# 64 of 512 columns of a copied score bank's exponential as a power of two times a polynomial, on VectorE and GpSimd

## The chip, the core and the metric

The kernel runs on one core of one Trainium2 chip. The metric is device microseconds of one execution: 1353.58 us for the kernel before, the median of three runs (1353.39 to 1354.35). The profile is of a further execution of the same kernel, taken by the hardware profiler; its own time is 1347.44 us, and its span, from the first to the last instruction, is 1345.6 us. Engines are named as in the profile: PE (TensorE matmul), PEld (TensorE weight load), ACT (ScalarE), DVE (VectorE), POOL (GpSimd), SP (SyncE, which here issues most DMAs).

## The reference

The output is a gated mix of a softmax attention and a mixture of experts over the same 2048 tokens of width 448. Only the attention's inner part is touched by the change.

```python
def _A_ref(x, wqkv, wo):                       # B = 1, S = 2048, D = 448, H = 16, Dh = 28
    q, k, v = ...
    scores = jnp.einsum("bhqd,bhkd->bhqk", q, k) * scale      # scale = Dh ** -0.5
    p = _softmax(scores, axis=-1)
    o = jnp.einsum("bhqk,bhkd->bhqd", p, v)
    return ...(o) @ wo

def _B_ref(x, w_gate, w1, w2):                 # 8 experts, the best 2 of each token
    ...

g = _sigmoid((x * gate_w).sum(-1, keepdims=True))
return g * _A_ref(x, A_wqkv, A_wo) + (1 - g) * _B_ref(x, B_w_gate, B_w1, B_w2)
```

## The kernel before

The kernel has four stages one after the other. First the projections, the routing of tokens and a pass of query-key products that finds each query's largest score; then the eight experts (to about 833 us in the profile), beside which that pass of maxima goes on; then attention (to about 1306 us); then the output projection of the 16 blocks of 128 tokens, which is the tail.

**Units and steps.** Attention is cut into 16 units u: four groups g of four heads by four chunks qc of 512 queries. A unit has eight steps p, and a step takes two blocks of 128 keys for the four heads at once. So there are 128 steps m = 8u + p. For each of the two key blocks, `score_passes` (L733) runs three passes of four matmuls, one for each head in rows of its own of the array, into four PSUM banks of 128 keys by 512 queries. The query carries minus its largest score as an extra row, so the scores come out shifted and the exponential needs no further bias. Three of the four banks are one tile (`s0` for the first key block, `s1` for the second), the fourth is a single bank, `z0` or `z1` in turn.

**The exponentials of a step.** In `scores(m)` ACT takes the first block's single bank (L1173, 512 columns) and its triple (L1174, 1536 columns) straight from PSUM. The second block's single bank is copied to SBUF first, by DVE (L1175, tile `X`), which frees the bank early; ACT then takes the second triple (L1176) and last the copy (L1177, 512 columns from `X`). All eight results stand in `P`. ACT does nothing else in this stage.

**The sums.** `values(m)` multiplies the eight parts of `P` by the values (L1188) into a single bank, the one that `z0` of the next step's scores has just left; row 28 of each head's 32 is the sum of the exponentials. DVE adds the bank to `osb` (L1194, and L1192 where p is 0). That same bank is then the second single bank of the scores after.

**The order.** PE, ACT, DVE and POOL follow the order in which the code is written; SP's DMAs stand in its own queue in the order in which they are issued. The loop issues `scores(m + 1)`, then `beside(m)`, then `values(m)`. So on DVE a step is: the copy of step m+1, the operations of `beside(m)`, the sum of step m.

**What `beside` adds.** At p = 2, 4, 5, 6 one DVE operation of `routed` (L1073 twice, L1075, L1077), which combines the experts' rows of one token block; at p = 5 two gathers by POOL for the next unit (L1064). The unit before is finished in between: at p = 0 `collect_sums` writes the four sum rows to DRAM and reads them back as 128x16 (L1110, L1112); at p = 3 `invert_sums` takes the reciprocal on DVE (L1116) and writes it (L1117); at p = 4 `spread_sums` reads it back, spread over 32 rows for each head (L1122); at p = 7 `divide` multiplies `osb` by it (L1127) and sends the rows to `OT` by SP (L1137). These small DMAs are issued by POOL. At p = 0 of the units 5 to 8 DVE also splits a block of `wo` (L1057, L1058), and at p = 0, 1 and 3 of unit 15 a block of `OT` (L1086 and the helper's L180, L181). The keys, values and queries of what comes next are loaded by SP: a unit's queries at p = 7 of two units before (L719, L721), a group's keys at p = 3 and p = 6 of the last unit of the group before (L704, L707), its second half of values at p = 0 of its first unit (L691).

**The tail.** Each of the 16 blocks needs 22 matmuls (L1097), one DVE operation (L1100) and a DMA to the output; ACT and DVE split `OT` four blocks ahead. The last unit's sums are collected, inverted, spread and divided between these blocks, and blocks 12 to 15 need them.

Of the kernel before, what the change touches and what calls it, by code (L numbers as in the profile page):

```python
# [1 line left out]

# [6 lines left out]
F32 = mybir.dt.float32  # L9
F32R = mybir.dt.float32r  # L10
BF = mybir.dt.bfloat16
I32 = mybir.dt.int32
AF = mybir.ActivationFunctionType
ALU = mybir.AluOpType
# [21 lines left out]
S, D, H, DH, E, FF = 2048, 448, 16, 28, 8, 1792  # L36
# [13 lines left out]
SCALE = float(DH) ** -0.5  # L50
# [7 lines left out]
def bc(ap, shape):  # L58
    return ap.to_broadcast(shape)
# [3 lines left out]
def tile_gated_mha_moe(ctx: ExitStack, tc: tile.TileContext, x, xe_, xT, wv, wqk, wo, w1, w2, out):  # L63
    nc = tc.nc
# [10 lines left out]
    sum_d = dram.tile([NG * 4, 4, 512], F32, name="sum_d")  # L75
    inv_d = dram.tile([NG * 4, 4, 512], F32, name="inv_d")
# [200 lines left out]
    with ExitStack() as pa:  # L277
        sb = pa.enter_context(tc.tile_pool(name="pa_sb", bufs=1))
# [116 lines left out]
        for t in range(NT):  # L395
# [11 lines left out]
            if 7 <= t < 15:  # L407
                b, c = divmod(t - 7, 2)
# [3 lines left out]
                                        op=ALU.subtract)  # L412
# [325 lines left out]
    with ExitStack() as pb:  # L738
        sb1 = pb.enter_context(tc.tile_pool(name="pb_sb1", bufs=2, reuse_waits="tile"))
        sb = pb.enter_context(tc.tile_pool(name="pb_sb", bufs=2, reuse_waits="tile"))  # L740
# [159 lines left out]
        for e in range(E):  # L900
# [12 lines left out]
            for hf in range(2):  # L913
# [3 lines left out]
                for f in range(NH):  # L917
                    ft = hf * NH + f
                    p = e * NP + ft // 2
# [69 lines left out]
                for n_k, k in enumerate((4, 0, 1, 2, 3)):  # L989
# [12 lines left out]
                    for f in range(NH if k < 4 else 0):  # L1002
# [10 lines left out]
                        if hf == 1 and e + 1 < E and (f == 1 or f == 4 and n_k == 1):  # L1013
                            j = n_k if f == 1 and n_k > 1 else f // 4
# [27 lines left out]
    sb = ctx.enter_context(tc.tile_pool(name="pc_sb", bufs=2, reuse_waits="tile"))  # L1042
# [62 lines left out]
    def by_slices(d):  # L1105
        return d.rearrange("j (i n) -> (j i) n", n=16)

    def collect_sums(u):
        for j in range(4):
            nc.gpsimd.dma_start(sum_d[u, j:j + 1], accs[u][32 * j + DH:32 * j + DH + 1])  # L1110
        rc[u] = sb.tile([128, 16], F32, name="rc")
        nc.gpsimd.dma_start(rc[u], by_slices(sum_d[u]))  # L1112

    def invert_sums(u):
        r = rc.pop(u)
        nc.vector.reciprocal(r, r)  # L1116
        nc.gpsimd.dma_start(by_slices(inv_d[u]), r)  # L1117

    def spread_sums(u):
        rs[u] = sb.tile([128, 512], F32, name="rs")  # L1120
        for j in range(4):
            nc.gpsimd.dma_start(rs[u][32 * j:32 * j + 32], bc(inv_d[u, j:j + 1], [32, 512]))  # L1122

    def divide(u):
        g, qc = divmod(u, 4)
# [14 lines left out]

    ctx.enter_context(tc.manual_schedule(engines=MANUAL_E))
    NPR = NT // 2
    NU = 4 * NG
    b1s, halves, ygs, sums = {}, {}, {}, {}
    accs, rc, rs = {}, {}, {}
# [4 lines left out]
    def single(i):  # L1150
        return ps.tile([128, 512], F32, name=f"z{i % 2}")

    def triple(i):
        return ps.tile([128, 3, 512], F32, name=f"s{i}")
# [6 lines left out]
    def scores(m):  # L1161
        u, p = divmod(m, NPR)
        if p == 0 and u and u + 1 < NU:
            qs[u + 1] = load_q((u + 1) // 4, (u + 1) % 4)
        X = sb.tile([128, 512], F32, name="X")
        P = sb.tile([128, 8, 512], F32, name="P")
        z, t = [None] * 2, [None] * 2
        for i in range(2):
            kt = 2 * p + i
            z[i], t[i] = single(m + i), triple(i)  # L1170
            three = [t[i][:, j] for j in range(3)]
            score_passes(kt, held[u // 4][0][kt // 8], qs[u], three + [z[i]] if i else [z[i]] + three)
        nc.scalar.activation(P[:, 0], z[0], AF.Exp, scale=SCALE)  # L1173
        nc.scalar.activation(P[:, 1:4], t[0], AF.Exp, scale=SCALE)  # L1174
        nc.vector.tensor_copy(X, z[1])  # L1175
        nc.scalar.activation(P[:, 4:7], t[1], AF.Exp, scale=SCALE)  # L1176
        nc.scalar.activation(P[:, 7], X, AF.Exp, scale=SCALE)  # L1177
        Pc[m] = [P[:, i] for i in range(8)]

    def values(m):  # L1180
        u, p = divmod(m, NPR)
        P = Pc.pop(m)
        po = single(m + 1)
        for i in range(2):
            kt = 2 * p + i
            v = held[u // 4][1][kt // 8]
            for j in range(4):
                nc.tensor.matmul(po[32 * j:32 * j + 32], v[:, kt % 8, 32 * j:32 * j + 32], P[4 * i + j],  # L1188
                                 start=i == 0, stop=i == 1)
        if p == 0:  # L1190
            accs[u] = sb.tile([128, 512], F32, name="osb", bufs=3)
            nc.vector.tensor_copy(accs[u], po)  # L1192
        else:
            nc.vector.tensor_tensor(accs[u], po, accs[u], op=ALU.add)  # L1194

    def beside(m):
        u, p = divmod(m, NPR)
        g, qc = divmod(u, 4)
# [9 lines left out]
        if u and p == 0:  # L1208
            collect_sums(u - 1)
        if p == 5 and u + 1 < NU:  # L1210
            fetch_routed(u + 1)
# [15 lines left out]
    fetch_routed(0)  # L1227
    WHOLE_O = [(NU - 1, 0), (NU - 1, 1), (NU - 1, 3)]
    for m in range(NU * NPR):
        if m + 1 < NU * NPR:  # L1230
            scores(m + 1)
        beside(m)
        values(m)
    collect_sums(NU - 1)
    split_o(3, nc.scalar)

# [67 lines left out]
```

## Time and profile before

| what | us |
|---|---|
| median of three timed runs | 1353.58 |
| the profiled execution, its own time | 1347.44 |
| its span | 1345.60 |
| PE busy, share of the span | 1339.2, 100% |
| DVE busy | 927.7, 69% |
| ACT busy | 847.5, 63% |
| POOL busy | 617.1, 46% |
| in the 100 us from 1000 to 1100: PE, ACT | 100.0, 100.0 |
| in the same: DVE, POOL | 50.4, 24.0 |

The shares of the whole span mix stages. In the slices of the profile ACT is at 9 tenths in all from the 26th to the 38th, which is the attention, and at 3 to 6 tenths ahead of it; PE counts as busy nearly throughout, and its granted clock is full in all slices. Records of ACT and DVE can overlap: an instruction may begin before the record ahead of it has ended. So a step's length is read from the distance between the same instruction in two steps, not from a sum of durations.

### The profile page before, as it was taken

To read this page: it belongs to the slowest core of one execution; us is meant where nothing else is said; L and a number is where in the kernel's file an instruction comes from. 1 tells how busy PE (TensorE), PEld (TensorE's weight loads), DVE (VectorE), ACT (ScalarE), POOL (GpSimd) and SP (SyncE) were. 2 spreads that over 40 slices of the span, in tenths; PEclk is the share of its full clock that TensorE was granted. 3 is DMA by queue.
4 is the path that set the end of the run, shared out by engine and by line. 5 is a ranking of instruction groups with operands and counts; after the bars stand their busy time and mean duration, and the time that the engine had idled before them with its cause. 6 is when DMAs were issued, how large, how long until landed. Compare 5 with 4: busy or idle time off the path is not lost. (4 is left out here: it accounts for less than half of the span.)

```text
span 1345.6 us, 27214 instructions
## 1 busy us (share of the span) xinstructions
PE 1339.2 (100%) x10166; PEld 888.0 (66%) x10166; DVE 927.7 (69%) x1076; ACT 847.5 (63%) x1270; POOL 617.1 (46%) x661
## 2 busy tenths in 40 slices
PE   9999999999999999999999999999999999999998
PEld 8888788788887777777777777444444444444448
DVE  5736898888988888988898785444454544444465
ACT  5325354364354343543445535999999999999981
POOL 2123765676587577775777753122222222222220
PEclk9999999999999999999999999999999999999999
DMA  9887856753553465534655303223422422342213
GB/s 354 300 266 269 301 154 196 242 153 107 159 157 95 146 201 154 149 101 143 204 156 152 105 36 93 64 58 103 126 83 72 130 80 58 101 126 74 59 31 129
DMA packets 136278, 191.30 MB, mean 142 GB/s; under 512 B 23284, under 2 KB 102680, under 8 KB 135632
## 3 DMA queue, kind: packets, MB, share of 16 engines
q1 hardware_dynamic: 124992, 160.55, 38.6%
q0 software_dynamic: 11008, 28.76, 7.2%
q8 instruction: 80, 1.31, 0.4%
q14 instruction: 54, 0.44, 0.1%
q10 hardware_dynamic: 144, 0.23, 0.1%
HBM read 139.20 MB, written 60.74 MB: 149 GB/s over the span
## 5 line engine op out<-in xcount | busy, mean ns | idle before, releaser
L143 DVE TENSOR_REDUCE mp<-pm 128x3 f32<-128x1536 f32 (+1 forms) x301 | 508.9, 1733 | 11.0 <-PE pm L122 11.0
L1188 PE MATMUL z<-P,V 128*32 128x512 f32 x2032 | 244.7, 598 | 0.1
L1176 ACT ACTIVATE P<-s 128x1536 f32<-128x1536 f32 x127 | 199.2, 1568 | 0.0
L1174 ACT ACTIVATE P<-s 128x1536 f32<-128x1536 f32 x127 | 197.6, 1556 | 0.0
L1175 DVE COPY X<-z 128x512 f32<-128x512 f32 x127 | 87.9, 692 | 150.7 <-PE z L733 141.5
L733 PE MATMUL s<-Q,Kh 29*128 29x512 f32 x1524 | 187.7, 444 | 0.0
L733 PE MATMUL z<-Q,Kh 29*128 29x512 f32 x508 | 185.6, 444 | 0.0
L804 POOL TENSOR_TENSOR w2l<-w2r,w2h 128x448 fp32r<-128x448 f32 x112 | 129.4, 1156 | 119.2 <-ACT w2h L798 80.1
L1020 ACT ACTIVATE yo<-acc 128x448 f32<-128x448 f32 x64 | 34.9, 546 | 233.2 <-PE acc L1006 228.8
L1006 PE MATMUL acc<-w2h,hh 128*128 128x448 f32 x448 | 167.6, 374 | 0.3 <-PEq L818 0.3
L1006 PE MATMUL acc<-w2h,hl 128*128 128x448 f32 x448 | 166.5, 372 | 0.0
L1006 PE MATMUL acc<-w2l,hh 128*128 128x448 f32 x448 | 166.1, 371 | 0.0
L949 ACT ACTIVATE hf<-acc 128x512 f32<-128x512 f32 (+6 forms) x154 | 74.3, 482 | 137.9 <-PE acc L945 131.1
L136 DVE TENSOR_REDUCE mp<-acc 128x1 f32<-128x512 f32 x130 | 89.5, 688 | 85.0 <-PE pm L122 83.1
L813 POOL TENSOR_TENSOR hl<-hf,hh 128x512 fp32r<-128x512 f32 x112 | 145.1, 1295 | 1.0 <-ACT hh L952 1.0
L733 PEld LDWEIGHTS z<-Q,Kh 29*128 29x128 f32 x508 | 74.5, 183 | 106.5 <-DVE yg L1073 26.8
L1188 PEld LDWEIGHTS z<-P,V 128*32 128x32 f32 x2032 | 53.1, 109 | 130.1 <-issue 76.0
L945 PE MATMUL acc<-xeh,w1h 128*128 128x512 f32 (+3 forms) x408 | 136.8, 339 | 0.0
L1194 DVE TENSOR_TENSOR osb<-z,osb 128x512 f32<-128x512 f32 x112 | 77.4, 691 | 85.7 <-PE z L1188 85.6
L945 PE MATMUL acc<-xeh,w1l 128*128 128x512 f32 (+3 forms) x408 | 136.0, 338 | 0.0
L772 POOL TENSOR_TENSOR w1l<-w1r,w1h 128x1024 fp32r<-128x1024 f32 (+1 forms) x49 | 90.8, 1853 | 60.8 <-ACT w1h L766 47.1
L122 PE MATMUL pm<-khg,qg 28*128 28x512 f32 x894 | 110.5, 449 | 0.9 <-DVE lo L645 0.9
(221 smaller groups left out, 2704.7 us busy)
## 6 DMA issues: line engine op xcount, KB each, us to landing
w2r<-in_w_dram SPq DMA_DIRECT2D x112, 224.0 KB
w1r<-in_w_dram SPq DMA_DIRECT2D x56, 384.0 KB
ys_d<-zero_d SPq DMA_DIRECT2D x32, 448.0 KB
ys_d<-yo SPq DMA_DIRECT2D x64, 224.0 KB
x_d<-xf SPq DMA_DIRECT2D x115, 64.0 KB
qkh_d<-hi SPq DMA_DIRECT2D x28, 256.0 KB
qkl_d<-lo SPq DMA_DIRECT2D x28, 256.0 KB
w1r<-in_w_dram SPq DMA_DIRECT2D x112, 64.0 KB
```

The source lines that it names most:

```text
L122: nc.tensor.matmul(banks[n], qgs[g, qt // 4][rw, (qt % 4) * 128:(qt % 4 + 1) * 128], kh[g, kc][rw], start=True, stop=True)
L136: nc.vector.tensor_reduce(mp[:, o:o + 1], banks[0], axis=AX.X, op=ALU.max)
L143: nc.vector.tensor_reduce(mp[:, (o + lo) % 256:(o + lo) % 256 + hi - lo], pm[h][:, lo - 3 * h:hi - 3 * h], axis=AX.X, op=ALU.max)
L733: nc.tensor.matmul(banks[j], k[rw, ks], q[rw, c], start=i == 0, stop=i == 2)
L772: nc.gpsimd.tensor_tensor(l[:, :, half], r[:, :, half], h[:, :, half].bitcast(F32), op=ALU.subtract)
L804: nc.gpsimd.tensor_tensor(w2l, w2r, w2h.bitcast(F32), op=ALU.subtract)
L813: nc.gpsimd.tensor_tensor(hl, hf32, hh[:, 0:512].bitcast(F32), op=ALU.subtract)
L945: nc.tensor.matmul(pu[:, 0:HC], a, b[:, cs], start=i == 0, stop=i == len(mms) - 1)
L1006: nc.tensor.matmul(py[:n, 0:D], a[:, cs], b, start=i == 0, stop=i == 3 * NH - 1)
L1174: nc.scalar.activation(P[:, 1:4], t[0], AF.Exp, scale=SCALE)
L1176: nc.scalar.activation(P[:, 4:7], t[1], AF.Exp, scale=SCALE)
L1188: nc.tensor.matmul(po[32 * j:32 * j + 32], v[:, kt % 8, 32 * j:32 * j + 32], P[4 * i + j], start=i == 0, stop=i == 1)
```

## The change

The copy `X` becomes a multiplication and a maximum: it holds the score times SCALE and log2(e), so that the exponential is a power of two, and is kept at -126 or above. ACT's last operation of a step leaves out the first 64 of the 512 columns (its scale is ln 2 now). Those 64 columns are worked out by `power`, in two pieces:

- right behind the copy, DVE adds a large constant, which leaves the rounded exponent in the low bits (`u`), and takes the rounded minus the exact value (`g`); then POOL makes the first two coefficients of a polynomial in `g` (`r`, a multiplication and an addition), multiplies it by `g`, and makes the power of two itself (`e`) from `u` as an integer that is read as a float;
- behind the sum of step m, DVE does the rest for step m+1: three operations of (r + c) g, and (r + 1) times `e` into `P`.

So each of the steps 1 to 127 has six more operations of 64 columns on DVE and three on POOL, and ACT's instruction count stays. The ten small DMAs of a unit's sums (4 + 1 + 1 + 4) go from POOL's queue to SP's.

```diff
     def collect_sums(u):
         for j in range(4):
-            nc.gpsimd.dma_start(sum_d[u, j:j + 1], accs[u][32 * j + DH:32 * j + DH + 1])
+            nc.sync.dma_start(sum_d[u, j:j + 1], accs[u][32 * j + DH:32 * j + DH + 1])
         rc[u] = sb.tile([128, 16], F32, name="rc")
-        nc.gpsimd.dma_start(rc[u], by_slices(sum_d[u]))
+        nc.sync.dma_start(rc[u], by_slices(sum_d[u]))
...
-        nc.gpsimd.dma_start(by_slices(inv_d[u]), r)
+        nc.sync.dma_start(by_slices(inv_d[u]), r)
...
-            nc.gpsimd.dma_start(rs[u][32 * j:32 * j + 32], bc(inv_d[u, j:j + 1], [32, 512]))
+            nc.sync.dma_start(rs[u][32 * j:32 * j + 32], bc(inv_d[u, j:j + 1], [32, 512]))
...
+    PW = 64
+    ROUND = 1.5 * 2.0 ** 23 + 127.0
+    EXP2 = (1.0, -0.6931469775984714, 0.24022242084918496, -0.05550733744243862, 0.009671512660596779,
+            -0.0013264726899206907)
+    powers = {}
...
-        nc.vector.tensor_copy(X, z[1])
+        nc.vector.tensor_scalar(X, z[1], SCALE * math.log2(math.e), -126.0, op0=ALU.mult, op1=ALU.max)
         nc.scalar.activation(P[:, 4:7], t[1], AF.Exp, scale=SCALE)
-        nc.scalar.activation(P[:, 7], X, AF.Exp, scale=SCALE)
+        nc.scalar.activation(P[:, 7, PW:], X[:, PW:], AF.Exp, scale=math.log(2.0))
         Pc[m] = [P[:, i] for i in range(8)]
+        powers[m] = power(X[:, 0:PW], P[:, 7, 0:PW])
+        next(powers[m])
+
+    def power(x, to):
+        u, g, r = (sb.tile([128, PW], F32, name=f"p{c}") for c in "ugr")
+        e = sb.tile([128, PW], I32, name="pe2")
+        nc.vector.tensor_scalar(u, x, ROUND, None, op0=ALU.add)
+        nc.vector.scalar_tensor_tensor(g, u, ROUND, x, op0=ALU.subtract, op1=ALU.subtract)
+        nc.gpsimd.tensor_scalar(r, g, EXP2[5], EXP2[4], op0=ALU.mult, op1=ALU.add)
+        nc.gpsimd.tensor_tensor(r, r, g, op=ALU.mult)
+        nc.gpsimd.tensor_scalar(e, u, 1.5 * 2.0 ** 23, 2.0 ** 23, op0=ALU.subtract, op1=ALU.mult)
+        yield
+        for c in (3, 2, 1):
+            nc.vector.scalar_tensor_tensor(r, r, EXP2[c], g, op0=ALU.add, op1=ALU.mult)
+        nc.vector.scalar_tensor_tensor(to, r, 1.0, e.bitcast(F32), op0=ALU.add, op1=ALU.mult)
...
         beside(m)
         values(m)
+        if m + 1 in powers:
+            next(powers.pop(m + 1), None)
```

DVE's queue in unit 10, from the copy that stands ahead of L1077's operation (p = 6) to the division (p = 7). Before:

```order
L1175 COPY X_13769<-z0_13785 128x512
L1077 SCALAR_TENSOR_TENSOR b1_13609<-yg1_13354,coef_79,b1_13609 128x448
L1194 TENSOR_TENSOR osb_13527<-z1_13805,osb_13527 128x512
L1175 COPY X_13828<-z1_13844 128x512
L1127 TENSOR_TENSOR osb_13125<-osb_13125,rs_13703 128x512
```

The same place after the change, where `pu`, `pg`, `pr` and `pe2` are the tiles u, g, r and e of `power`:

```order
L1181 TENSOR_SCALAR X_14783<-z0_14799 128x512
L1191 TENSOR_SCALAR pu_14818<-X_14783 128x64
L1192 SCALAR_TENSOR_TENSOR pg_14819<-pu_14818,X_14783 128x64
L1078 SCALAR_TENSOR_TENSOR b1_14580<-yg1_14260,coef_79,b1_14580 128x448
L1215 TENSOR_TENSOR osb_14472<-z1_14828,osb_14472 128x512
L1198 SCALAR_TENSOR_TENSOR pr_14820<-pr_14820,pg_14819 128x64 x3
L1199 SCALAR_TENSOR_TENSOR P_14784<-pr_14820,pe2_14821 128x64
L1181 TENSOR_SCALAR X_14855<-z1_14871 128x512
L1191 TENSOR_SCALAR pu_14890<-X_14855 128x64
L1192 SCALAR_TENSOR_TENSOR pg_14891<-pu_14890,X_14855 128x64
L1128 TENSOR_TENSOR osb_13966<-osb_13966,rs_14700 128x512
```

Two small operations now stand between the copy and the operation of `beside`, and four between the sum and the next copy.

POOL's queue at the gathers of the same unit (p = 5). Before:

```order
L1122 DMA rs_13703<-inv_d_69 32x512 x4
L1064 DMA yg0_13754<-ys_d_76,slot_i_80 128x896
L1064 DMA yg1_13756<-ys_d_76,slot_i_80 128x896
L1110 DMA sum_d_68<-osb_13527 16x1x32 x4
L1112 DMA rc_13918<-sum_d_68 128x16
```

After:

```order
L1193 TENSOR_SCALAR pr_14757<-pg_14756 128x64
L1194 TENSOR_TENSOR pr_14757<-pr_14757,pg_14756 128x64
L1195 TENSOR_SCALAR pe2_14758<-pu_14755 128x64
L1065 DMA yg0_14764<-ys_d_76,slot_i_80 128x896
L1065 DMA yg1_14766<-ys_d_76,slot_i_80 128x896
L1193 TENSOR_SCALAR pr_14820<-pg_14819 128x64
L1194 TENSOR_TENSOR pr_14820<-pr_14820,pg_14819 128x64
L1195 TENSOR_SCALAR pe2_14821<-pu_14818 128x64
```

The queue held only DMA issues in this stage; now each step has three operations, and of the DMAs the two gathers are left.

SP's queue where group 2 begins (p = 7 of unit 7 to p = 4 of unit 8), after the change:

```order
L720 DMA Q_13826<-qkh_d_63 28x512 x4
L720 DMA Q_13826<-qkl_d_64 28x512 x4
L722 DMA Q_13826<-m_d_65 1x512 x4
L1138 DMA OT_9778<-osb_12914 16x512
L1138 DMA OT_9778<-osb_12914 12x512
L1138 DMA OT_9778<-osb_12914 28x512 x3
L692 DMA V1_13947<-v_d_67 128x8x128
L1111 DMA sum_d_68<-osb_13424 1x512 x4
L1113 DMA rc_13953<-sum_d_68 128x16
L1118 DMA inv_d_69<-rc_13953 128x16
L1123 DMA rs_14194<-inv_d_69 32x512 x4
```

The last four rows are the moved ones: unit 7's sums stand behind the queries of unit 9, the rows of unit 6 for `OT` and the values of the group, where they stood alone on POOL before.

## Rows read from the trace of the kernel before

**Rows 1.** The page's 40 slices of the span, ACT's row: the busy share of each slice in tenths.

```profile
ACT  5325354364354343543445535999999999999981
```

**Rows 2.** The timeline of ACT over one step of attention: start, duration, engine, line, operation.

```profile
1012.46 0.76 ACT L1177 ACTIVATE P<-X 128x512 f32<-128x512 f32 x1
1012.98 0.72 ACT L1173 ACTIVATE P<-z 128x512 f32<-128x512 f32 x1
1013.48 1.56 ACT L1174 ACTIVATE P<-s 128x1536 f32<-128x1536 f32 x1
1014.81 1.57 ACT L1176 ACTIVATE P<-s 128x1536 f32<-128x1536 f32 x1
1016.14 0.76 ACT L1177 ACTIVATE P<-X 128x512 f32<-128x512 f32 x1
```

**Rows 3.** The timeline of PE and DVE over the same step, p = 0 of unit 6; in brackets the idle time ahead and what ended it.

```profile
1013.75 1.92 PE L1188 MATMUL z<-P,V 128*32 128x512 f32 x16
1013.88 0.69 DVE L1175 COPY X<-z 128x512 f32<-128x512 f32 x1 [1.13 <-PE z L733]
...
1014.90 0.62 DVE L1058 TENSOR_TENSOR wo_l<-wo_r,wo_h 128x448 fp32r<-128x448 f32 x1
...
1015.74 0.69 DVE L1192 COPY osb<-z 128x512 f32<-128x512 f32 x1 [0.22 <-PE z L1188]
...
1016.49 0.18 PEld L733 LDWEIGHTS z<-Q,Kh 29*128 29x128 f32 x1
...
1017.44 1.92 PE L1188 MATMUL z<-P,V 128*32 128x512 f32 x16
```

**Rows 4.** The timeline of PE and DVE in unit 15, from p = 0, where DVE splits a block of `OT`, over p = 1 to the value matmuls of p = 2.

```profile
1283.01 1.92 PE L1188 MATMUL z<-P,V 128*32 128x512 f32 x16
...
1285.26 0.69 DVE L1194 TENSOR_TENSOR osb<-z,osb 128x512 f32<-128x512 f32 x1
...
1286.90 1.92 PE L1188 MATMUL z<-P,V 128*32 128x512 f32 x16
...
1288.89 0.69 DVE L1194 TENSOR_TENSOR osb<-z,osb 128x512 f32<-128x512 f32 x1 [0.59 <-PE z L1188]
...
1289.63 0.18 PEld L733 LDWEIGHTS z<-Q,Kh 29*128 29x128 f32 x1
...
1290.53 1.92 PE L1188 MATMUL z<-P,V 128*32 128x512 f32 x16
```

**Rows 5.** The timeline of DVE in the routing: pairs of small operations, the second of which reads the first's result (50.48, 50.74) or does not (59.05, 59.14).

```profile
50.48 0.22 DVE L485 TENSOR_TENSOR ahead<-key 128x64 f32<-128x64 f32 x1
50.74 0.22 DVE L488 TENSOR_REDUCE pos<-ahead 128x8 f32<-128x64 f32 x1
...
59.05 0.18 DVE L534 TENSOR_SCALAR ti<-slot_i 128x32 int32<-128x32 int32 x1
59.14 0.17 DVE L537 TENSOR_SCALAR bi<-slot_i 128x32 int32<-128x32 int32 x1
```

**Rows 6.** Groups of instructions from 900 to 1200 us, shapes apart: two operations of `beside`, busy us and mean ns.

```profile
L1073 DVE TENSOR_TENSOR yg<-yg 128x448 f32<-128x448 f32 x21 | 12.9, 616 | 0.0
L1077 DVE SCALAR_TENSOR_TENSOR b<-yg,coef,b 128x448 f32<-128x448 f32 x10 | 6.8, 676 | 0.0
```

**Rows 7.** Groups of POOL's instructions over the whole span, shapes apart: operations of two inputs at 384 and at 64 columns, busy us and mean ns.

```profile
L791 POOL TENSOR_TENSOR xel<-xg,xeh 128x384 fp32r<-128x384 f32 x28 | 28.4, 1016 | 3.8 <-issue 1.9 <-POOL xeh L792 1.0
...
L792 POOL TENSOR_TENSOR xeh<-xg,xeh 64x64 fp32r<-64x64 f32 x1 | 0.3, 318 | 0.1
```

**Rows 8.** The timelines of POOL and DVE at the start of the kernel: POOL's two one-input operations, both of 128 columns, and what DVE ran beside them.

```profile
1.26 0.23 DVE L306 TENSOR_SCALAR ident<-jp 128x128 f32<-128x128 f32 x1 [1.26 <-POOL jp L304]
...
1.37 0.57 POOL L319 TENSOR_SCALAR tri<-jp 128x128 bf16<-128x128 f32 x1
...
3.54 0.61 POOL L338 TENSOR_SCALAR iob<-jp,iop 128x128 bf16<-128x128 f32 x1
...
4.00 0.29 DVE L382 TENSOR_TENSOR xl<-xt,xh 128x128 fp32r<-128x128 f32 x1 [2.51 <-ACT xh L380]
```

**Rows 9.** The timelines of DVE and POOL in the routing: one POOL operation beside a DVE operation with two inputs in SBUF (62.08 beside 61.91), and the same one later without such an operation (69.89).

```profile
61.91 1.22 DVE L549 TENSOR_TENSOR xt<-iob,bb 128x1024 bf16<-128x1024 bf16 x1
...
62.08 1.95 POOL L556 TENSOR_TENSOR xt<-ot,iot 128x512 bf16<-128x512 bf16 x1 [24.02 <-DVE ot L553]
...
69.89 1.05 POOL L556 TENSOR_TENSOR xt<-ot,iot 128x512 bf16<-128x512 bf16 x1 [0.69 <-issue]
```

**Rows 10.** The timelines of SP and DVE where group 3 begins (p = 7 of unit 11 to p = 3 of unit 12), and, as the last row, what the answer on line L1110, the writes of the sums, says of them.

```profile
1197.51 0.47 SPq L691 DMA_DIRECT2D V<-v_d  x1
...
1202.57 0.24 DVE L1116 RECIPROCAL rc<-rc 128x16 f32<-128x16 f32 x1
...
DMA to landing us min/median/max: 1.7/1.9/3.1
```

**Rows 11.** The timelines of the tail: SP's sends of unit 14 to `OT`, DVE's reciprocal of unit 15, ACT's wait for unit 15's rows in `OT`; and, as the last row, PE's matmuls of blocks 12 and 13 in the chain that ended last, in order of time.

```profile
1304.97 6.10 SPq L1137 DMA_DIRECT2D OT<-osb  x8
...
1314.44 0.25 DVE L1116 RECIPROCAL rc<-rc 128x16 f32<-128x16 f32 x1
...
1329.56 1.93 ACT L1084 ACTIVATE oh<-OT 128x512 fp32r<-128x512 f32 x3 [4.80 <-DMA OT<-osb]
...
1333.02 4.49 PE s L1097 x22
```

More of the change, by code (lines that the diff above doesn't have):

```diff
@@ L1 @@
+import math
 from contextlib import ExitStack
```

## The prediction, as it was made before the changed kernel ran

> **What bounds the kernel now.** I read the slices first, then ACT's timeline, then PE's and DVE's, and last the waits. The slices put the whole change into one stage: ACT is at 9 tenths only in the attention [rows 1], so only there can relief of ACT be worth anything. There the ends of ACT's records, not their starts, show what an operation takes, since an instruction begins before the one ahead has ended [rows 2]. The ends are 1013.22 (L1177), 1013.70 (L1173), 1015.04 (L1174), 1016.38 (L1176) and 1016.90 (L1177): distances of 0.48, 1.34, 1.34 and 0.52, together 3.68 us, with no gap. PE's step, from one start of the value matmuls to the next, is 1017.44 - 1013.75 = 3.69 us [rows 3]. So ACT sets the step: PE counts as busy throughout, but its value matmuls start 0.05 us after ACT's L1173 has ended. A column costs ACT (1.34 - 0.48) / 1024 = 0.00084 us.
>
> What is late next has to be known, since ACT's gain is only worth what PE can follow. A second loop runs through DVE: values, sum into `osb`, second single bank, values. In [rows 3] the sum starts 1.99 us behind the values, the weights of the bank's scores are loaded at 2.74, the next values start at 3.69. Unit 15 shows this loop without ACT's brake. There the sum of p = 0 came late, so ACT had caught up, and the step after it took 1290.53 - 1286.90 = 3.63 us, with the sum at 1.99 and the weights at 2.73 [rows 4]. So PE and DVE can go at 3.63, and not below it while this chain stands.
>
> **The change, part by part.** All terms are made against the profiled execution (its own time 1347.44, its span 1345.60, 1.84 outside the span); the median of the runs lies 6.14 above it, and I carry the difference over unchanged.
>
> *ACT's columns.* 64 x 0.00084 = 0.054 us less in each of 127 steps; ACT's step becomes 3.63, just the 3.63 of the other loop. Gain 127 x 0.053 = 6.7 us. Had the other loop nothing to say it would be no more, since the instruction count of ACT stays. From here on every delay of the sum in `osb` counts in full: before, 0.05 us of it a step was free.
>
> *The copy.* One more arithmetic operation in the same pass over PSUM. The copy takes 0.69 [rows 3], and so does the sum with two inputs [rows 4]; I take 0.69, and above 0.75 it would begin to be felt below.
>
> *The two small operations behind the copy.* 64 columns with a wait on the result ahead take 0.22 and a pause of 0.04; 32 columns take 0.18 [rows 5]. I take 0.19 for `u` and 0.22 for `g`, so DVE is free 0.49 us later than before. An independent operation starts 0.09 before the end of the one ahead [rows 5]. In a step, the copy ends at 0.82 behind the values, `g` at 1.31; the longest single operation of `beside`, 0.68 [rows 6], then runs from 1.22 to 1.90, and the sum is due at 1.99, held up by the value matmuls. So in the ordinary step these two operations are hidden, with 0.18 to spare. They are not where DVE had more to do. At p = 0 of units 5 to 8 the split of `wo` ends at 1015.52, 0.22 ahead of the sum [rows 3]: 0.49 - 0.22 - 0.09, about 0.2 us, four times, +0.8. In the three split steps of unit 15 the sum is late already (2.25 in place of 1.99, rows at 1283.01 and 1285.26 [rows 4]), and the 0.49 adds itself nearly whole: 3 x 0.45 = +1.35.
>
> *POOL's three operations.* No row shows them. The two-input one: 0.32 at 64 columns [rows 7]. The two one-input ones: 0.57 and 0.61 at 128 columns [rows 8] is above; below is the same 0.57 without the 0.12 for which L306 ran beside it, and without 64 columns at the (1016 - 318) / 320 = 2.2 ns that a column costs POOL with two inputs [rows 7]: 0.57 - 0.12 - 0.14 = 0.31. Bounds 0.25 to 0.55; I take 0.36, nearer the lower end because half of the columns must cost something. All three together about 1.05 us.
>
> They also meet DVE. L556 took 1.05 alone and 1.95 beside L549, a DVE operation with two inputs in SBUF that ran until 63.13: POOL stood still until DVE was done [rows 9]. The Trainium skill (SBUF — State Buffer, Who interferes with whom) says the same and more: a port that the two share, held for a whole instruction by whichever comes first, for DVE operations with two SBUF inputs too. For POOL behind DVE the trace agrees (0.9 us lost in L556). For DVE behind POOL it does not show it: L382, with two inputs, ran its 0.29 at 4.00 while L338 was on POOL until 4.15 [rows 8].
>
> So in a step with an operation of `beside` (p = 2, 4, 5, 6, 7), POOL starts when that operation ends, at 1.90, and is done at about 3.0; `r` is there at 2.65. DVE's last four operations can start at 2.60 (sum at 1.99, its 0.69, the overlap). Their chain is 4 x 0.26 = 1.04, so they end at 3.64 to 3.70, and the next copy is due at 3.63 + 0.13 = 3.76: hidden. If DVE is held until POOL is done (3.0), they end at 4.04 and the copy comes 0.2 late; two such steps in a row, p = 6 and 7, use up the 0.18 to spare and the sum begins to slip, some 0.1 us a unit. I take half of what 15 units would then lose, with a share for the split steps: +0.6, range 0 to the rival below. `P` of these columns is ready by 4.1 at the latest; the value matmul that reads it last starts near 3.63 + 0.9.
>
> *The DMAs on SP.* They now stand behind the queries, `OT` and the values. The tightest place is the start of a group. There the load of the values was issued until 1197.98 [rows 10]; four writes of the sums at some 0.3 each, 1.9 until they have landed, the read back and as much again: 1197.98 + 1.2 + 1.9 + 0.3 + 1.9 = 1203.3, against a reciprocal that was at 1202.57 [rows 10] and, behind two more operations of DVE, can wait until about 1203.4 before it delays the sum. Just in time; with the slowest landing of the row, 3.1, it is 1 to 2 us late, three times. I take +0.4, range 0 to 4. Elsewhere in a unit the read back has 4 us in hand. SP itself waits for nothing that others behind it need earlier.
>
> In the tail, the writes of unit 15's sums come behind SP's sends until 1311.07 [rows 11] and the read back behind three output blocks: the reciprocal moves from 1314.4 to about 1317, all that follows by 2 to 3 us, and ACT's split of block 12 from 1329.56 to about 1332.3. With its 0.63 and DVE's share it is ready near 1333, where PE starts block 12 at 1333.0 [rows 11]. +0.4, range 0 to 3.
>
> Sum: -6.7 + 0.8 + 1.35 + 0.6 + 0.4 + 0.4 = -3.15 us. 1353.58 - 3.15 = 1350.4.
>
> **The rivals.** First, **the gain is given back**: POOL at about 0.42 for each one-input operation, DVE held by it, or one to two microseconds more at SP. The step's chain of copy, `g`, `beside`, POOL, four operations is then 2.33 + 0.68 + 2 x 0.42 = 3.85 at p = 6 and 7 (2.33: 1.18 to `g`, 0.32 and its pauses, 0.92 of the four, less the overlap), the sum slips 0.2 a unit: -3.15 + 2 to 3 makes 1352 to 1353.5. For it speaks that the spare time at every one of these places is only 0.1 to 0.2 us; against it L382 and that half of the steps have slack to recover.
>
> Second, **slower: DVE's and POOL's chain becomes the step**. It decides from about 0.40 us for POOL's one-input operation with DVE held. At 0.52 the chain is 2.33 + 0.62 + 1.04 = 3.99 at p = 4, 3.82 at p = 5 (its operation is 0.17 shorter), 4.05 at p = 6 and 7; over 3.63 that is 0.36 + 0.19 + 0.42 + 0.42 = 1.39, less 0.3 in hand, about 1.1 a unit, 15 units 16 us: 1353.6 + 16 - 4 = about 1366; at 0.45, where it only begins, 1357. For it: 0.57 at 128 columns, if most of it does not depend on the columns. The Trainium skill (GPSIMD Engine Reference, Engine selection) calls one-input operations there roughly line-rate; an estimate by it, with 64 columns at 0.8 ns off the 0.57, is 0.52 us, the case just priced. Against it: L382 again, and 0.32 for two inputs at the same width, beside which 0.52 for one would be odd.
>
> Third, **slower through SP**: landings of 3 us in place of 1.9 at the three group starts, and PE waiting for block 12: +4 +3 on what is else -3.95, so 1356 to 1357.
>
> **How the numbers follow.** 0.2% is 2.7 us, about what a measurement can tell from no change. The forecast, a gain of 2.7 to 5 us: 0.48. Given back: 0.30. Slower by DVE's and POOL's chain: 0.17; by SP: 0.05. The best case is the sum with only the split steps against it, -4.55 and 0.3 for ACT's part: 1348.7. Upward the range takes in the given-back case and the beginning of the slower ones, to 1357. The forecast's own range is 1348.7 to 1350.9. Faster 0.48, same 0.30, slower 0.22.
>
> **What the profile after would show.** Right: L1183, ACT's shortened operation, with ends 0.46 to 0.47 behind L1182's in place of 0.52; steps of 3.63 to 3.64 us at p = 1 and 3; POOL's one-input operations near 0.36; the sum at 1.99 behind the values in all but seven steps; DVE's chain of four ended before the next copy; no wait of L1117's reciprocal for a DMA but at the start of a group. Wrong: ACT idle ahead of L1179, POOL at 0.45 or more, the first of the four operations held until POOL has ended, steps of 3.8 or more at p = 6 and 7, or a wait of PE at block 12.

## The result: slower by 0.7%

The changed kernel takes 1360.78 us, the median of six runs (1358.59 to 1366.85), beside 1352.64 us for the kernel before (six runs, 1350.1 to 1354.35): a ratio of 1.0067, 95% interval 1.0043 to 1.0091, or 6 to 12 us more. The prediction of 1350.4 has the wrong sign, and 1360.78 lies above its range. The profiled execution of the changed kernel is the longest of its six (its own time 1366.85, span 1365.10), and that of the kernel before (1347.44) is shorter than each of its six timed runs, so the traces show the losses larger than they are on the whole. The timed runs of the experiments give their size, the trace their place.

| | before | after |
|---|---|---|
| span of the profiled execution, us | 1345.6 | 1365.1 |
| first value matmul of the attention | 836.57 | 839.56 |
| from the values of m = 1 to those of m = 126 | 461.4 | 476.4 |
| DVE busy, us | 927.7 | 1084.1 |
| POOL busy, us | 617.1 | 688.5 |

Of the 19.5 us between the spans, 3.0 arose ahead of the attention, where the change touches nothing, 15.0 between two starts of value matmuls in it, and the rest behind them: the last sum of the attention is 0.6 later, and the tail 0.8 longer. The page's slices of ACT and of the granted clock already show that something stands still:

```profile
ACT  5325354355254443444434445999899989999971
PEclk9999999999999999999999999999899999999999
```

Before, ACT was at 9 in every slice of the attention but the last [rows 1]. Now it falls to 8 in the 29th and the 33rd, and the clock to 8 in the 29th.

**The ordinary step** is what the change was to make faster. The timeline of all engines over the step of p = 1 of unit 9:

```profile
1121.61 1.92 PE L1209 MATMUL z<-P,V 128*32 128x512 f32 x16
1121.79 0.69 DVE L1181 TENSOR_SCALAR X<-z 128x512 f32<-128x512 f32 x1
1122.52 0.20 DVE L1191 TENSOR_SCALAR pu<-X 128x64 f32<-128x64 f32 x1
1122.69 1.46 ACT L1182 ACTIVATE P<-s 128x1536 f32<-128x1536 f32 x1
1122.75 0.22 DVE L1192 SCALAR_TENSOR_TENSOR pg<-pu,X 128x64 f32<-128x64 f32 x1
1123.05 0.24 POOL L1193 TENSOR_SCALAR pr<-pg 128x64 f32<-128x64 f32 x1 [2.48 <-DVE pg L1192]
1123.38 0.32 POOL L1194 TENSOR_TENSOR pr<-pr,pg 128x64 f32<-128x64 f32 x1
1123.63 0.69 DVE L1215 TENSOR_TENSOR osb<-z,osb 128x512 f32<-128x512 f32 x1 [0.66 <-PE z L1209]
1123.79 0.43 POOL L1195 TENSOR_SCALAR pe<-pu 128x64 int32<-128x64 f32 x1
1124.03 0.59 ACT L1183 ACTIVATE P<-X 128x448 f32<-128x448 f32 x1
1124.24 0.73 DVE L1198 SCALAR_TENSOR_TENSOR pr<-pr,pg 128x64 f32<-128x64 f32 x3
1124.53 0.60 ACT L1179 ACTIVATE P<-z 128x512 f32<-128x512 f32 x1
1125.07 0.23 DVE L1199 SCALAR_TENSOR_TENSOR P<-pr,pe 128x64 f32<-128x64 f32 x1
1125.27 0.64 PE L1209 MATMUL z<-P,V 128*32 128x512 f32 x4
```

It is 3.66 us, against 3.69 before [rows 3], not the 3.63 of the forecast. ACT's shortened L1183 ends 0.47 behind L1182 (1124.62 and 1124.15), as forecast; but the sum starts 2.02 behind the values in place of 1.99, and L1179 takes its whole 0.60 where L1173 had begun under the operation ahead [rows 2]. POOL is quicker than I took it to be, the copy is 0.69 as before, and DVE is idle for 0.66 us ahead of the sum.

**The start of a group** is where the time went. SP, DVE and PE in p = 2 to 5 of unit 8:

```profile
1093.51 0.47 SPq L692 DMA_DIRECT2D V<-v_d  x1
1094.09 1.28 SPq L1111 DMA_DIRECT2D sum_d<-osb  x4
1094.54 1.92 PE L1209 MATMUL z<-P,V 128*32 128x512 f32 x16
1097.84 0.36 SPq L1113 DMA_DIRECT2D rc<-sum_d  x1
1099.73 0.25 DVE L1117 RECIPROCAL rc<-rc 128x16 f32<-128x16 f32 x1 [3.82 <-DMA rc<-sum_d]
1101.66 3.36 PE L1209 MATMUL z<-P,V 128*32 128x512 f32 x16
1106.77 0.64 PE L1209 MATMUL z<-P,V 128*32 128x512 f32 x4
```

Where the reciprocal ran in time before [rows 10], it holds DVE for 3.82 us, and the sum, the single bank and PE with it: the step takes 7.12. The next takes 5.11, since its value matmuls last 3.36 us in place of 1.92. The table of the two stretches (PE, PEld, DVE, ACT and POOL busy, PE's granted clock, DMA share, GB/s) says why:

```profile
1098.00:1101.60 3.60, 1.02 (x9) 0.49 (x9) 1.61 (x6) 1.62 (x3) 0.00 (x0) 0.94 0.07 11
1101.60:1104.00 2.40, 2.40 (x13) 0.59 (x16) 1.65 (x4) 1.69 (x2) 0.81 (x2) 0.50 0.16 55
```

PE was busy for 1.02 of 3.60 us, and then ran at half its clock (1.2 GHz). Unit 4 shows the same (3.3 us of waiting, steps of 7.09 and 5.69), unit 12 a wait of 1.7 and one step of 4.95. Over 3.69 a step, the five steps make 11.5 of the 15.0 us.

**At p = 6** the sum is late in each of the 15 units that have gathers, here in unit 8:

```profile
1111.01 0.97 POOL L1065 DMA_INDIRECT yg<-ys_d,slot_i  x1 [0.30 <-issue]
1111.70 0.68 DVE L1078 SCALAR_TENSOR_TENSOR b<-yg,coef,b 128x448 f32<-128x448 f32 x1
1112.04 0.44 POOL L1193 TENSOR_SCALAR pr<-pg 128x64 f32<-128x64 f32 x1
1112.65 0.69 DVE L1215 TENSOR_TENSOR osb<-z,osb 128x512 f32<-128x512 f32 x1 [0.27 <-PE z L1209]
```

It starts 2.23 behind the values of 1110.42 and makes the step 3.88. DVE had been free for 0.27 us, and by their records, whose ends are modelled, the value matmuls were over at 1112.34. What DVE stood for is PE's semaphore, a counter that PE raises when matmuls are done and for which the sum waits (`<-PE z L1209`): the trace's records of its updates have the last one at 2.20 behind these values, where it is at 1.99 in p = 5 of the same unit, and in both steps the sum starts 0.03 behind it. PE's own next matmuls start on time, 1.85 behind the values in both. The 15 steps of this kind are 2.3 us longer than 15 steps before. The rest of the 15.0: the three `OT` splits +1.5, the four `wo` splits +0.8, the second step of the attention +1.4 and one step of unit 1 +0.3; the 96 steps that are left took 2.8 us less.

### The profile page after: what moved, and what is told of

Same layout as the page of the kernel before. It is cut to its first block, busy times and chain, and to the rows that moved or that the text cites. A ratio compares the mean times of both kernels' runs of the same rounds, so it can differ in the third digit from the quotient of the medians.

```text
span 1365.1 us, 28455 instructions
## 1 busy us (share of the span) xinstructions
PE 1348.1 (99%) x10166; PEld 901.4 (66%) x10166; DVE 1084.1 (79%) x1838; ACT 845.8 (62%) x1270; POOL 688.5 (50%) x882
## 5 line engine op out<-in xcount | busy, mean ns | idle before, releaser
L1209 PE MATMUL z<-P,V 128*32 128x512 f32 x2032 | 249.3, 605 | 0.7 <-DVE P L1199 0.6
L1193 POOL TENSOR_SCALAR pr<-pg 128x64 f32<-128x64 f32 x127 | 54.0, 425 | 267.7 <-DVE pg L1192 266.7
L1182 ACT ACTIVATE P<-s 128x1536 f32<-128x1536 f32 x127 | 185.5, 1461 | 3.9 <-PE s L734 3.9
L734 PE MATMUL s<-Q,Kh 29*128 29x512 f32 x1524 | 183.8, 433 | 0.0
L1180 ACT ACTIVATE P<-s 128x1536 f32<-128x1536 f32 x127 | 183.8, 1447 | 0.0
L1209 PEld LDWEIGHTS z<-P,V 128*32 128x32 f32 x2032 | 53.6, 110 | 127.5 <-issue 79.8
L1181 DVE TENSOR_SCALAR X<-z 128x512 f32<-128x512 f32 x127 | 87.8, 692 | 26.0 <-PE s L734 8.1
```

The costliest lines, as they stand in the source:

```text
L734: nc.tensor.matmul(banks[j], k[rw, ks], q[rw, c], start=i == 0, stop=i == 2)
```

## The experiments

Theory S: the loss is the place of the small DMAs on SP. Theory P, my second rival: POOL's three operations and DVE's hold each other. Theory G, formed after the first four runs: POOL's gathers hold DVE (what the traces show them to delay is PE's signal to DVE, as told below).

| run | median us | ratio to before, 95% |
|---|---|---|
| changed kernel | 1360.78 | 1.0067 [1.0043, 1.0091] |
| DMAs back on POOL | 1380.83 | 1.0205 [1.0189, 1.0221] |
| DMAs on SP alone | 1357.10 | 1.0031 [1.0018, 1.0043] |
| ACT 448 columns alone | 1350.62 | 0.9987 [0.9977, 0.9998] |
| ACT 384 columns alone | 1350.53 | 0.9980 [0.9970, 0.9990] |
| no POOL operations, DMAs on POOL | 1360.60 | 1.0057 [1.0042, 1.0073] |
| late reciprocal | 1355.05 | 1.0018 [1.0009, 1.0027] |
| late reciprocal, no gathers | 1352.32 | 0.9993 [0.9984, 1.0002] |
| chosen steps | 1349.75 | 0.9977 [0.9966, 0.9988] |
| split gathers | 1347.80 | 0.9962 [0.9948, 0.9975] |
| split gathers, more power | 1348.50 | 0.9964 [0.9950, 0.9978] |

### The small DMAs back on POOL

```diff
-            nc.sync.dma_start(sum_d[u, j:j + 1], accs[u][32 * j + DH:32 * j + DH + 1])
+            nc.gpsimd.dma_start(sum_d[u, j:j + 1], accs[u][32 * j + DH:32 * j + DH + 1])
...
```

> The changed kernel with the ten small DMAs of a unit issued by POOL again; the nine operations of the power stay. Theory S (SP's queue): the stalls at the starts of groups 1 to 3, 5.5, 4.9 and 1.3 us in the changed kernel's trace, come from the DMAs' place on SP and vanish. But then POOL's three operations of a step stand behind POOL's own issues and their landings (2.03 + 2.15 + 0.57 us at p = 0, 0.55 + 1.4 + 2.0 at p = 3 and 4 in the trace of before), and r comes 1 to 2 us late at one or two steps of each of 15 units: 15 to 40 us, so 1365 to 1390 us in all. Theory P (POOL's operations hold DVE's): where the DMAs are issued matters little; about 1361, with the stalls still there in some form. If the stalls go and nothing queues on POOL: about 1349.

1380.83 us. The reciprocal's waits are gone, and POOL's queue takes their place. POOL and DVE in unit 2, p = 0 to 2:

```profile
902.16 2.08 POOL L1111 DMA_DIRECT2D sum_d<-osb  x4
905.98 0.56 POOL L1113 DMA_DIRECT2D rc<-sum_d  x1 [1.73 <-DMA sum_d<-osb]
906.62 0.23 POOL L1193 TENSOR_SCALAR pr<-pg 128x64 f32<-128x64 f32 x1
...
907.29 0.74 DVE L1198 SCALAR_TENSOR_TENSOR pr<-pr,pg 128x64 f32<-128x64 f32 x3 [1.30 <-POOL pr L1194]
```

POOL issues for 2.08, waits 1.73 for the landing, and only then makes `r`, for which DVE stands 1.30 us. So with the power on POOL the small DMAs can't stay there, and this run can't by itself say what they cost on SP.

### The small DMAs on SP, and nothing else

The kernel before with `nc.sync` in place of `nc.gpsimd` for the ten DMAs.

> The kernel before with only the ten DMAs of a unit moved to SP; no power. Theory S: the same stalls at the three group starts, 1 to 5.5 us each, so 5 to 12 us above the kernel before: 1358 to 1365. Theory P: nothing, 1352.6, since ACT sets the step and POOL runs nothing beside DVE.

1357.10 us, 4.2 us slower (2.4 to 5.8): a little under what S gave, and P's "nothing" is out. The starts of groups 2 and 3 have steps of 5.18 and 5.49. DVE and PE at the first of these:

```profile
1088.91 1.92 PE L1188 MATMUL z<-P,V 128*32 128x512 f32 x16
...
1092.34 0.25 DVE L1116 RECIPROCAL rc<-rc 128x16 f32<-128x16 f32 x1 [2.62 <-DMA rc<-sum_d]
...
1094.09 1.92 PE L1188 MATMUL z<-P,V 128*32 128x512 f32 x16
```

Here the value matmuls behind the wait last 1.92: the clock held. In its trace the three group starts make 3.4 us. Another 3.3 us stand in the second and third step of the attention (5.91 and 4.77), beside the gathers with which it begins; the changed kernel has 1.4 us of this, and the run with 448 columns, whose small DMAs are on POOL, 1.8. So not all of the 4.2 us can be put to the group starts.

### ACT's relief alone, 448 and 384 columns

```diff
-        nc.scalar.activation(P[:, 7], X, AF.Exp, scale=SCALE)
+        nc.scalar.activation(P[:, 7, 64:], X[:, 64:], AF.Exp, scale=SCALE)
+        rest[m] = P[:, 7, 0:64], X[:, 0:64]
...
+        if m + 1 in rest:
+            nc.vector.tensor_copy(*rest.pop(m + 1))
```

> The kernel before, DMAs on POOL, with ACT's last operation of 448 columns; the other 64 columns' exponential is left out and one DVE copy behind the sum puts the scores there. It is the floor for what the relief of ACT can give. If the step is 3.63 as in unit 15 of the kernel before, 127 x 0.053 = 6.7 us less: 1346. If PE's scores of the single bank, ACT's operation on them and the value matmuls are a loop of 3.655, as the changed kernel's ordinary steps, 127 x 0.033 = 4.2 less: 1348.4.

> ACT's last operation with 384 columns, the other 128 columns' exponential left out (one DVE copy in its place), DMAs on POOL as in the kernel before. It asks what sets the ordinary step after the change. If ACT still did, twice the columns would give 3.60 us a step, 11 us less than the kernel before, 1342. If the step is held by PE (values, scores of the single bank, ACT's operation on them, values), it stays 3.655, and the time is that of the run with 448 columns, 1350.6.

1350.62 and 1350.53: 64 more columns off ACT bring nothing, and the ordinary step is 3.65 to 3.67 in both. But the 4.2 us that such a step promises are not reached: 448 columns gave 1.8 (0.3 to 3.1). In its trace p = 5, where POOL's two gathers stand, is 3.70 to 4.03 in 11 of 15 units, 1.4 us in all, and the second step is 5.41. With 384 columns, ACT's timeline in unit 9:

```profile
1121.08 0.53 ACT L1178 ACTIVATE P<-X 128x384 f32<-128x384 f32 x1
1121.58 0.60 ACT L1174 ACTIVATE P<-z 128x512 f32<-128x512 f32 x1
```

L1174 starts 0.50 behind L1178, as in the changed kernel (1124.03, 1124.53), though L1178 is shorter by 64 columns. So ACT's columns no longer set the step. By the trace it is the loop values, scores of the single banks, values, with the sum and ACT's L1174 between.

### POOL's three operations left out

```diff
-        nc.gpsimd.tensor_scalar(r, g, EXP2[5], EXP2[4], op0=ALU.mult, op1=ALU.add)
-        nc.gpsimd.tensor_tensor(r, r, g, op=ALU.mult)
-        nc.gpsimd.tensor_scalar(e, u, 1.5 * 2.0 ** 23, 2.0 ** 23, op0=ALU.subtract, op1=ALU.mult)
```

> The changed kernel with the DMAs on POOL and POOL's three operations left out (DVE's last four read a constant in place of r and e). Theory P: what POOL's operations held is free again: the sum at 1.99 behind the values in place of 2.02, the 0.21 us at p = 6 and most of what the split steps lost are gone, 1346 to 1348. If DVE's own six operations are the cost: steps of 3.655, p = 6 still 0.2 longer, the three OT splits 0.6 each: 1352.6 - 4.2 + 3.2 + 0.9 + 1.7 = about 1354.

1360.60, above what either theory gave; with nothing of the power on POOL, P can't be the cause of this run's loss. What POOL's operations cost in the changed kernel the run can't tell, since its DMAs and gathers stand elsewhere. The trace's loss is at p = 5 now, 0.35 to 1.0 us in 13 units, where POOL has only gathers to do. POOL, ACT and DVE in unit 4:

```profile
975.75 0.97 POOL L1065 DMA_INDIRECT yg<-ys_d,slot_i  x1 [0.30 <-issue]
...
977.11 1.45 ACT L1184 ACTIVATE P<-s 128x1536 f32<-128x1536 f32 x1 [0.27 <-PE z L734]
977.22 0.69 DVE L1183 TENSOR_SCALAR X<-z 128x512 f32<-128x512 f32 x1 [1.61 <-PE z L734]
```

By their records the matmuls of the scores that L1183 reads ended at 975.70; it started half a microsecond after the gather's end. But it was not DVE that was held. The lines of ACT and DVE name PE as what ended the idle time: the records have PE's semaphore raised at 977.09 and 977.12, and ACT, which waits for it too, started at the same moment. L1183 stands 0.10 behind the update, as in other steps (0.08 and 0.18 behind the values). So beside a gather PE's signal comes late, and whoever waits for it starts late. The delay, and the place at which p = 6 is late in the changed kernel, made theory G.

### The reciprocal two steps later at the starts of groups

```diff
-        if u and p == 3:
+        if u and p == (3 if qc else 5):
             invert_sums(u - 1)
-        if u and p == 4:
+        if u and p == (4 if qc else 5):
             spread_sums(u - 1)
```

> The changed kernel, all nine operations and the DMAs on SP; only in the first unit of groups 1 to 3 the reciprocal and its two DMAs come two steps later (p = 5 in place of 3 and 4). Theory S, that the loss at the group starts is the reciprocal at the head of DVE's queue waiting for a landing: the three stalls (5.5, 4.9 and 1.3 us in the trace of the changed kernel) are gone, nothing takes their place, and the attention is about 11 us shorter: 1350 to 1353. Theory P, that DVE and POOL together are the loss: within 2 us of the changed kernel, 1359 to 1362.

1355.05, 5.7 us less than the changed kernel by the medians and 6.6 by the ratios ((1.0067 - 1.0018) x 1352.6); 2 us above S's range, since other losses stay. PE and DVE at the start of group 2:

```profile
1094.51 1.92 PE L1209 MATMUL z<-P,V 128*32 128x512 f32 x16
1095.79 0.25 DVE L1117 RECIPROCAL rc<-rc 128x16 f32<-128x16 f32 x1
```

No wait stands at the reciprocal, and every step of p = 2 to 5 there is 3.65 or 3.66. S is shown, as the largest part of the loss.

### The gathers left out

```diff
     def fetch_routed(t):
+        if t:
+            ygs[t] = first[0]
+            return
```

> The run above with POOL's gathers of the units 1 to 15 left out (all units combine the rows of unit 0). It asks what makes the sum 0.1 to 0.2 us late at p = 6. Theory G, the gathers hold DVE: the sum is at 2.02 behind the values at p = 6 too, and 15 x 0.2 = 3 us less than the run above. Theory P, POOL's first operation beside the operation of beside holds the sum: p = 6 stays at 2.1 to 2.25, the time that of the run above.

1352.32, 3.4 us less than the run above by the ratios. In 14 of 15 units p = 6 is 3.65 or 3.66. DVE and POOL there, in unit 8, behind the values of 1098.24:

```profile
1099.52 0.68 DVE L1084 SCALAR_TENSOR_TENSOR b<-yg,coef,b 128x448 f32<-128x448 f32 x1
1099.68 0.62 POOL L1199 TENSOR_SCALAR pr<-pg 128x64 f32<-128x64 f32 x1 [2.28 <-DVE pg L1198]
1100.25 0.69 DVE L1221 TENSOR_TENSOR osb<-z,osb 128x512 f32<-128x512 f32 x1
```

POOL's operation, 0.24 alone, stretches to 0.62 until the one of `beside` has ended; the sum comes 2.01 behind the values. Here POOL waits for DVE, and the sum doesn't wait for POOL's operations. So the lateness at p = 6 goes with the gathers, and P is out for the changed kernel too.

### A version for the steps where it pays

```diff
+    FULL = {8 * u + 6 for u in range(16)} | {8 * u for u in range(5, 9)} | {0, 1, 120, 121, 123}
...
+        if m - 1 in FULL:
+            nc.scalar.activation(P[:, 7], X, AF.Exp, scale=math.log(2.0))
+            return
```

> A version that should beat both: the late reciprocal of the first run, the last unit's small DMAs on POOL, and no power in the 25 steps in which DVE has more to do or a gather stands beside it (p = 6 of each unit, the split steps, the first two); ACT does all 512 columns there. By the traces: some 100 steps at 3.655 in place of 3.688 is 3.4 us less than the kernel before, and nothing lost elsewhere: 1349 to 1350. Under theory P the remaining steps still lose at p = 2, 4, 5 and 7 and it is no better than 1353.

1349.75: it beats both kernels, and the split steps are at about their old lengths. (The late reciprocal is that of the run named so in the table.) But p = 6 is still 3.75 to 4.24, without the power in it. It also holds steps with and without the power side by side. PE and DVE at p = 1 of unit 6, whose `P` is ACT's alone, and at p = 2:

```profile
1019.23 1.92 PE L1213 MATMUL z<-P,V 128*32 128x512 f32 x16
1021.22 0.69 DVE L1219 TENSOR_TENSOR osb<-z,osb 128x512 f32<-128x512 f32 x1 [0.64 <-PE z L1213]
1022.86 1.92 PE L1213 MATMUL z<-P,V 128*32 128x512 f32 x16
1024.88 0.69 DVE L1219 TENSOR_TENSOR osb<-z,osb 128x512 f32<-128x512 f32 x1
```

The sum is at 1.99 and the step 3.63 in the first; at 2.02 and 3.65 in the second. In PE's queue the second group of value matmuls has one wait more, on DVE ahead of the eighth part of `P`:

```
L1213 MATMUL z_11148<-P,V_9768 32x512 [waits Activation_49]
L1213 MATMUL z_11148<-P,V_9768 32x512 x6
L1213 MATMUL z_11148<-P,V_9768 32x512 [waits DVE_49]
L1213 MATMUL z_11220<-P,V_9768 32x512 [waits Activation_49]
L1213 MATMUL z_11220<-P,V_9768 32x512 x7
```

(The first three lines are a step with the power, the last two one without.) So the 0.025 us go with the second writer of that part, as they do in the run with 448 columns, which has one DVE copy and no power. It is not the wait that costs them: the value matmuls start at the same distances in both steps, the last at 1.33. But with the wait the seventh part's matmul raises PE's semaphore for the parts so far and the eighth's raises it once more, recorded at 1.95 and 1.99 behind the values, where without it there is one update, at 1.97. The sum starts 0.02 behind the last update in both.

### The gathers split over two steps

```diff
-        if p == 5 and u + 1 < NU:
-            fetch_routed(u + 1)
+        if p in (5, 6) and u + 1 < NU:
+            fetch_routed(u + 1, (p - 5,))
```

> The version with chosen steps, but the two gathers of the next unit come one at p = 5 and one at p = 6, each behind POOL's operations of its step. In the version with chosen steps the second gather stood at 0.59 to 1.55 behind the values of p = 6 and the sum there was 0.1 to 0.6 late in every unit, without any operation of the power beside it. Theory G: with no gather ending just ahead of the sum, p = 6 falls from 3.87 to 3.66, 15 x 0.2 = 3 us less: 1346 to 1347. If any gather near the sum holds it, the loss moves to p = 7 or doubles: 1350 to 1352.

> The same with split gathers, and the power also at p = 6 (116 steps with it). Theory G: p = 6 at 3.66 with the power too, so within 0.5 us of the run above. If POOL's first operation beside L1078 of beside holds the sum, p = 6 is 0.1 to 0.2 longer than in the run above, 1.5 to 3 us more.

1347.80 and 1348.50, 4.9 and 4.2 us below the 1352.71 of the kernel before in these rounds, the shortest of all. The first missed its mechanism: without the power at p = 6 POOL has nothing to do ahead of the second gather, which starts as early as ever, and p = 6 stays at 3.75 to 4.20. In the second POOL's three operations push it back (3.15 behind the values in unit 9), and p = 6 is 3.65 or 3.66 in 12 of 15 units, with the power. In units 4, 8 and 12, where DVE's reciprocal is at p = 5, the first gather stands 0.08 later than in the others, PE's update for the copy comes 0.57 late again, and p = 6 is 4.06 to 4.08. The two times don't differ by more than their intervals.

## Why the prediction was wrong

| term | forecast, us | in the trace |
|---|---|---|
| ACT's relief | -6.7 (0.053 a step) | 0.033 a step |
| splits of `wo` | +0.8 | +0.8 |
| splits of `OT` | +1.35 | +1.5 |
| DVE and POOL, p = 2 to 7 | +0.6 | +2.3, by the gathers |
| SP at the group starts | +0.4 | +11.5 (5 to 7 timed) |
| tail | +0.4 | +0.4 at block 12, +0.8 at the end |

**The step that failed is the DMAs on SP**, and in it three things. "SP itself waits for nothing that others behind it need earlier" is wrong. An issue on SP waits for the landing of the DMA eight places ahead of it, since eight completion semaphores are used in turn. At the start of a group the queries of two units on thus wait for keys: those issued at 1085.01 for the keys that were issued at 1076.99. The view of SP's own waits, of group 2's start:

```profile
SPq L720 <- DMA Kh<-qkh_d: 2.6, 1, 2.6
```

So the values of the group, behind the queries and the rows for `OT`, were issued 10.3 us after the point at which L1179 ended for the group's second step (1093.51 and 1083.19), where the same stood 6.8 after it in [rows 10] (1197.51 and 1190.7), and 6.3 at group 2 of the kernel before:

```profile
1071.99 0.72 ACT L1173 ACTIVATE P<-z 128x512 f32<-128x512 f32 x1
...
1078.98 0.47 SPq L691 DMA_DIRECT2D V<-v_d  x1
```

I had taken SP's time from before, for a queue that the change had altered. Why the keys landed later was not tried and stays open. Second, "1.9 until they have landed" was the median of POOL's writes; the writes on SP took until 1097.84 from 1094.09, 3.75 in place of my 3.1 for issue and landing. Third, I priced a late reciprocal by its delay alone. PE stood behind it, its granted clock fell to half, and the step behind cost another 1.4 and 2.0 us over 3.69. The rival "slower through SP" had the place and half of the mechanism (late landings, but not the late issue nor the clock) and a chance of 0.05, with +4 for three starts where the trace shows 11.5.

**The relief of ACT** was right in kind and mis-sized. I took the 3.63 of unit 15 [rows 4] for the loop of PE and DVE (its rows are of p = 1, 2 and 3, not of 0, 1 and 2), but there `P` had one writer. With two, PE's last update comes 0.025 later, and the loop is 3.655. Of 6.7 us, 4.2 were there to be had; the run with 448 columns gives 0.3 to 3.1, and its trace shows 3.2 us lost beside gathers (p = 5 and the second step).

**The second rival was wrong**, and with it the price of POOL. Alone its first operation takes 0.24, just under my lower bound, the one with an integer result 0.43, the two-input one 0.32 as in [rows 7]; in a step without an operation of `beside` `r` is there at 2.09 behind the values. In the steps with one, for which I had 2.65, it is there at 2.2 to 2.7, since POOL's first operation stretches there, and all three are done at 2.7 to 3.2, about the 3.0 of the forecast. They didn't hold the sum: at p = 2 and 5 it stands at 2.02 in every unit. The estimate of 0.52 by the Trainium skill (GPSIMD Engine Reference, Engine selection) is far off for the first and nearer for the one with the integer result; the measurement decides. On the port the trace agrees with [rows 9] again: at p = 7 POOL's first operation stands still beside DVE's division, and the sum doesn't wait for it.

```profile
1145.09 0.69 DVE L1128 TENSOR_TENSOR osb<-osb,rs 128x512 f32<-128x512 f32 x1
1145.12 0.77 POOL L1193 TENSOR_SCALAR pr<-pg 128x64 f32<-128x64 f32 x1 [2.25 <-DVE pg L1192]
1145.70 0.69 DVE L1215 TENSOR_TENSOR osb<-z,osb 128x512 f32<-128x512 f32 x1
```

**The gathers were missing from the sum.** They were not moved in the code, but they follow three new operations in POOL's queue, and so came to stand ahead of the sum of p = 6: 2.3 us in the trace, 3.4 by the timed runs. They are not harmless in their old place either: in the run with 448 columns, where POOL's queue is that of before, 1.4 us are lost beside them at p = 5, while in the kernel before every step at p = 4 and 5 of the units 0 to 14 took 3.68 or 3.69. The share that I had put there for POOL's operations was right in place and wrong in cause.

**What held**: `u` and `g` at 0.20 and 0.22, hidden in the ordinary step; both kinds of split steps, priced by the queue of DVE. The timeline of PE and DVE at p = 1 of unit 15, as in [rows 4]:

```profile
1299.94 1.92 PE L1209 MATMUL z<-P,V 128*32 128x512 f32 x16
...
1302.59 0.69 DVE L1215 TENSOR_TENSOR osb<-z,osb 128x512 f32<-128x512 f32 x1
...
1304.22 1.06 PE L1209 MATMUL z<-P,V 128*32 128x512 f32 x8
```

The sum is 2.65 behind the values where it was 2.25, and the step 4.28 where it was 3.89.

In the tail the reciprocal ran at 1335.07, 10.6 behind the last sum at 1324.51, where it was 8.5 behind that sum, at 1305.9, before [rows 11]; block 12 started 27.5 behind it (1351.99), against 27.1. That is the forecast's 2 to 3 us for the one and 0.4 for the other.

## What to carry to other kernels

Moving DMAs to another queue changes when everything behind them is issued: take the new queue's times from the rows around the move, with the waits for its completion semaphores, and not the old queue's with the new DMAs added at the end. An operation at the head of an in-order engine's queue that waits for a landing should stand where a late landing costs nothing; two steps later it cost 0.2 to 0.3 us a time at p = 6 and gave back more than half of the loss. And new work on an engine also moves what follows it there: here it pushed an untouched gather to where it hurt.

## What the runs showed of the hardware that was not expected

- After PE had been busy for 1.02 of 3.60 us, its granted clock was 0.50 in the next 2.40 us and back at 1.00 from 1107 on; sixteen value matmuls took 3.36 us in place of 1.92. Behind a DVE wait of 2.62 us, in the run with the DMAs on SP alone, they took 1.92.
- Beside a gather on POOL, PE's signal to the engines that wait for it can come late: in the run without POOL's operations the updates stand at 977.09 and 977.12, with matmuls that ended at 975.70 by their records and a gather that ended at 976.72, and DVE (977.22) and ACT (977.11) started right behind. In the changed kernel the delay at p = 6 is 0.08 to 0.25 us (updates at 2.07 to 2.24 in place of 1.99), and without the gathers it is gone. The Trainium skill (SBUF — State Buffer, Who interferes with whom) says that a DVE instruction with at most one SBUF input outside the two-port modes does not contend with GpSimd; the 1.61 us for which DVE was idle do not speak against that, since they ended with PE's signal. In the kernel before, the steps beside the gathers at p = 4 and 5 took 3.68 or 3.69, as the others. What in a gather delays the signal was not tried and stays open.
- A second update of PE's semaphore at the end of sixteen value matmuls shifts what follows them by 0.025 to 0.03 us (updates at 1.95 and 1.99 in place of one at 1.97, the sum at 2.02 in place of 1.99).
- POOL's one-input operation on 128x64 took 0.24 us with a float result (a multiplication and an addition) and 0.43 with an integer one (a subtraction and a multiplication).
